# An offline-searched order of all instructions, butterflies over four row tiles, and final sums copied by ScalarE

## The chip, the cores and the metric

The kernel runs on one core of one Trainium2 chip. The metric is the device time of one execution in microseconds (us), given as the median of several executions on the same chip. The span in a profile runs from the first to the last instruction; in the runs of this case the time is 1.8 to 2.1 us longer than the span. The profile also gives the granted clock of TensorE, 1.00 being full rate. An execution is called slow when it is more than 1.5% above the fastest of its kernel; such executions are told, but not compared.

## The reference

```python
def reference(A_x, A_w_r, A_w_i, B_x, B_w_gate, B_w_up, B_w_down):
    xn = layernorm(A_x)                                  # x: 1 x 2048 x 640, bf16
    X = rfft2(xn.astype(float32)) * (A_w_r + 1j * A_w_i) # filter: 2048 x 321
    a = irfft2(X).astype(bfloat16)
    h = (xn @ B_w_gate) * (xn @ B_w_up)                  # 640 -> 1536
    return A_x + a + h @ B_w_down                        # 1536 -> 640
```

(The original has helpers for the Fourier transforms and makes random inputs.)

There are thus two branches on the same normalised x. The gate/up/down branch is plain matrix products. The spectral branch does the two-dimensional Fourier transform as a few stages: butterflies on VectorE, small products with tables on TensorE, a multiplication by the filter, and the same backwards.

## The kernel before

Every piece of work is a task: a name, the engines that can do it, an estimated duration for each, what it reads and writes, and a function that emits the instructions. A list scheduler in the program then decides order, engine and PSUM bank, always taking the task with the best priority among those that can start soon:

```python
def plan(self, nbanks=8, filler_deadline=0.0):
    ...
    while nsch < ntot:
        ...                                   # candidates: earliest start per engine
            slack = self.slack.get(e_, 100.0)
            ...
            for c in lst:
                if c is hc or c[1] <= hc[0] + slack:
                    k = (c[0], c[3].prio, c[3].tid)
        ...
        t.eng = e; t.start = est; order[e].append(t)
```

The order so found is emitted as it stands; each engine works through its list, and a task that has to wait holds up all behind it on its engine.

At the start 40 matmuls on zeros warm TensorE up, and "fillers" (four matmuls of 64 columns each) run where it would idle:

```python
dma("ld_sm0", v_sm[:, 0, :], d_sm[:, 0, :], 128 * 256, ..., prio=0.002, q="act")   # identity, 32 KB
...
for fi in range(opts.get("nfill", 70)):       # 11 of them find a place: 44 matmuls
    ...
nwarm = opts.get("nwarm", 10)                 # 4 * nwarm matmuls of 128 columns
```

The spectral stage, for each of 32 groups q: a product C, the multiplication by the filter on VectorE (WM), negated copies (NG, NS), and ten inverse products IA. The products of WM lie so that the stationary operand of eight of the ten takes every fourth element:

```python
def em_wm(...):                               # VectorE, 2 x 256 and 130 results
    xh = ps[:, bk, 0:256].rearrange("p (k h m) -> p h m k", k=4, h=2)[:, h]
    wv = wg[:, :, 0:320].rearrange("p w (m k) -> p w m k", k=10)
    wv = wv[:, :, :, 1:5] if h == 0 else wv[:, :, :, 9:5:-1]
    dst = yg[:, 578:1090].rearrange("p (w h m k) -> p h w m k", w=2, h=2, k=4)[:, h]
    c.e.tensor_tensor(dst, xh.unsqueeze(1).to_broadcast([128, 2, 32, 4]), wv, _OP.mult)
    ...
def em_ia(...):
    for k in range(5):
        if k < 4:
            l1, l2 = yg[:, 578 + k:1090:4], yg[:, 322 + k:834:4]
        else:
            l1, l2 = yg[:, 0:128], yg[:, 128:256]
        c.e.matmul(dst, l1, v_ti[:, q, 0, :], start=True, stop=False)
        ins = c.e.matmul(dst, l2, v_ti[:, q, 1, :], start=False, stop=True)
```

Butterflies go over two row tiles at a time, and each final sum is read from PSUM by VectorE, in two or three pieces for each of 16 row tiles:

```python
for g in range(8):
    b = 2 * g                                 # forward butterflies: 14 instructions a group
...
def em_f1(...):                               # FIN: PSUM + x -> out
    return c.e.tensor_tensor(v_out[:, a % 2, sl3], ps[:, bk, 0:n], v_xr[:, xs, sl3], _OP.add)
```

Of the kernel before, what the change touches and what calls it, by code (L numbers as in the profile page):

```python
# [17 lines left out]
_DMA_ISSUE = 500.0  # L18


class _Task(object):
    __slots__ = ("tid", "name", "engs", "dur", "emit", "prio", "deps", "nleft", "succ", "bank", "frees",
                 "freers", "eng", "start", "end", "seq", "units", "nbytes", "semkey", "semval", "cls", "vc",
                 "waits")
# [47 lines left out]
class _Sched(object):  # L72
    def __init__(self):
        self.tasks = []
        self.bufs = []
        self.caps = {}
        self.window = 250.0
        self.affinity = 600.0
        self.dma_bw = _DMA_BW
        self.slack = {"pe": 1000.0, "act": 300.0, "dve": 400.0, "pool": 100.0, "sp": 0.0}  # L80
        self.order = None
        self.urgent = ()
        self.makespan = 0.0
# [71 lines left out]
    def plan(self, nbanks=8, filler_deadline=0.0):  # L155
        tasks = self.tasks
        for t in tasks:
            t.succ = []
        for t in tasks:
            t.deps.discard(t)  # L160
            for d in t.deps:
                d.succ.append(t)
            t.nleft = len(t.deps)
        eng_free = dict((e, _START) for e in _ENGS)
        seq = dict((e, 0) for e in _ENGS)
        banks = [[0.0, None] for _ in range(nbanks)]
        held_by_cls = {}
        avail = [t for t in tasks if t.nleft == 0]
        pending_free = {}
        for t in tasks:  # L170
            if t.bank is not None:
                if not t.freers:
                    raise RuntimeError("task %s takes banks but nothing frees them" % t.name)
                pending_free[t.tid] = len(t.freers)
        free_end = {}
        dma_pipe = 0.0
        order = dict((e, []) for e in _ENGS)
        nsch = 0
        ntot = len(tasks)
        dropped = []  # L180

        def choose(kind):
            best = None
            if kind == "pair":
                for k in range(0, nbanks, 2):
                    a_, b_ = banks[k], banks[k + 1]
                    if a_[0] is None or b_[0] is None:
                        continue
                    ft_ = max(a_[0], b_[0])
                    if best is None or ft_ < best[0]:  # L190
                        best = (ft_, k)
            else:
                for k in range(nbanks):
                    st = banks[k]
                    if st[0] is None:
                        continue
                    partner = banks[k ^ 1]
                    pen = 0.0 if partner[0] is None else 1.0
                    key = (pen, st[0])
                    if best is None or key < best[2]:  # L200
                        best = (st[0], k, key)
            return best

        def release(p):
            k0 = p.units[1]
            nb = 2 if p.units[0] == "pair" else 1
            for k in range(k0, k0 + nb):
                banks[k][0] = free_end[p.tid]
                banks[k][1] = list(p.freers)
            held_by_cls[p.cls] -= 1  # L210

        while nsch < ntot:
            cands = []
            for t in avail:
                unit_choice = None
                bank_ready = 0.0
                if t.bank is not None:
                    cap = self.caps.get(t.cls)
                    if cap is not None and held_by_cls.get(t.cls, 0) >= cap:
                        continue  # L220
                    ch = choose(t.bank)
                    if ch is None:
                        continue
                    unit_choice = (t.bank, ch[1])
                    bank_ready = ch[0]
                    if bank_ready > 0.0:
                        bank_ready += _XLAT["pe"]
                best = None
                for ei, e in enumerate(t.engs):
                    est = eng_free[e]  # L230
                    for d in t.deps:
                        lat = _SLAT[e] if d.eng == e and not d.nbytes else _XLAT[e]
                        if d.eng == e and e == "pe":
                            lat = -_TAIL[e]
                        de = d.end + lat
                        if de > est:
                            est = de
                    if bank_ready > est:
                        est = bank_ready
                    fin = est + t.dur[e]  # L240
                    score = fin + (self.affinity if ei > 0 else 0.0)
                    if best is None or score < best[3]:
                        best = (est, fin, e, score)
                cands.append((best[0], best[1], best[2], t, unit_choice))
            real = [c for c in cands if c[3].cls != "fill"]
            if not cands or (not real and nsch + len([a_ for a_ in avail if a_.cls == "fill"]) < ntot
                             and not any(c[3].cls == "fill" for c in cands)):
                raise RuntimeError("scheduler deadlock: %d/%d scheduled, avail=%s" % (
                    nsch, ntot, [a_.name for a_ in avail][:10]))
            pick = None  # L250
            by_eng = {}
            for c in cands:
                by_eng.setdefault(c[2], []).append(c)
            for e_ in by_eng:
                lst = by_eng[e_]
                hb = None
                for c in lst:
                    k = (c[3].prio, c[0], c[3].tid)
                    if hb is None or k < hb[0]:
                        hb = (k, c)  # L260
                hc = hb[1]
                slack = self.slack.get(e_, 100.0)
                if hc[3].name in self.urgent:
                    slack = 100.0
                ch_ = None
                for c in lst:
                    if c is hc or c[1] <= hc[0] + slack:
                        k = (c[0], c[3].prio, c[3].tid)
                        if ch_ is None or k < ch_[0]:
                            ch_ = (k, c)  # L270
                c = ch_[1]
                k = (c[0], c[3].prio, c[3].tid)
                if pick is None or k < pick[0]:
                    pick = (k, c)
            est, fin, e, t, unit_choice = pick[1]
            if t.cls == "fill" and (est > filler_deadline or not real):
                for f in [a_ for a_ in avail if a_.cls == "fill"]:
                    avail.remove(f)
                    dropped.append(f)
                    nsch += 1  # L280
                    for s_ in f.succ:
                        s_.deps.discard(f)
                        s_.nleft -= 1
                        if s_.nleft == 0:
                            avail.append(s_)
                continue
            t.eng = e
            t.start = est
            if t.nbytes:
                issue_end = est + t.dur[e]  # L290
                ds = max(issue_end + _DMA_LEAD, dma_pipe)
                de = ds + t.nbytes / self.dma_bw
                dma_pipe = de
                t.end = de + _DMA_LAT
                eng_free[e] = issue_end
            else:
                t.end = fin + _TAIL[e]
                eng_free[e] = fin
                seq[e] += 1
            t.seq = seq[e]  # L300
            order[e].append(t)
            if unit_choice is not None:
                k0 = unit_choice[1]
                nb = 2 if unit_choice[0] == "pair" else 1
                for k in range(k0, k0 + nb):
                    st = banks[k]
                    if st[1] is not None:
                        for fr in st[1]:
                            t.deps.add(fr)
                    st[0] = None  # L310
                t.units = unit_choice
                held_by_cls[t.cls] = held_by_cls.get(t.cls, 0) + 1
            if t.bank is not None and t in t.freers:
                pending_free[t.tid] -= 1
                fe = free_end.get(t.tid, 0.0)
                if t.end > fe:
                    free_end[t.tid] = t.end
                if pending_free[t.tid] == 0:
                    release(t)
            for p in t.frees:  # L320
                pending_free[p.tid] -= 1
                fe = free_end.get(p.tid, 0.0)
                if t.end > fe:
                    free_end[p.tid] = t.end
# [8 lines left out]
        for f in dropped:  # L333
            self.tasks.remove(f)
# [48 lines left out]
_D = 640  # L383
# [966 lines left out]
```

## Time and profile before

| | before |
|---|---|
| time | 204.6 us (204.3 to 205.0), three executions |
| span of the profiled execution | 202.8 us, clock 1.00 |
| busy shares TensorE / VectorE / ScalarE / GpSimd | 98 / 89 / 63 / 16% |
| first 512-column product starts | 22.94 us |
| last matmul starts | 200.26 us |

The lines that carry the reading are in the prediction below.

### The profile page before, as it was taken

To read this page: it belongs to the slowest core of one execution; us is meant where nothing else is said; L and a number is where in the kernel's file an instruction comes from. 1 tells how busy PE (TensorE), PEld (TensorE's weight loads), DVE (VectorE), ACT (ScalarE), POOL (GpSimd) and SP (SyncE) were. 2 spreads that over 40 slices of the span, in tenths; PEclk is the share of its full clock that TensorE was granted. 3 is DMA by queue.
4 is the path that set the end of the run, shared out by engine and by line. 5 is a ranking of instruction groups with operands and counts; after the bars stand their busy time and mean duration, and the time that the engine had idled before them with its cause. 6 is when DMAs were issued, how large, how long until landed. Compare 5 with 4: busy or idle time off the path is not lost.

```text
span 202.8 us, 4769 instructions
## 1 busy us (share of the span) xinstructions
PE 198.0 (98%) x1785; PEld 128.1 (63%) x1785; DVE 179.5 (89%) x511; ACT 127.5 (63%) x277; POOL 32.0 (16%) x108
## 2 busy tenths in 40 slices
PE   7999999999999999899999999999999999999995
PEld 7987644454444555556666666667777767777774
DVE  3599999999999997697988898864999999999983
ACT  3678899999975776869999999987611220200000
POOL 0000000000000000075754675453000000000000
DMA  6999983031161597605354444004313332332222
GB/s 183 300 341 378 377 80 65 3 65 32 32 63 39 112 276 194 197 14 132 74 145 114 103 102 127 0 5 136 92 32 97 106 107 66 113 90 81 93 65 65
DMA packets 31542, 23.82 MB, mean 117 GB/s; under 512 B 10528, under 2 KB 29472, under 8 KB 31392
## 3 DMA queue, kind: packets, MB, share of 16 engines
q1 hardware_dynamic: 30720, 23.16, 43.5%
q10 hardware_dynamic: 800, 0.36, 0.6%
q8 instruction: 14, 0.23, 0.5%
q14 instruction: 8, 0.07, 0.1%
HBM read 18.92 MB, written 2.62 MB: 106 GB/s over the span
## 4 chain that ended last, share of the span: by engine, by line
PE 85%; DVE 5%; SPq 4%; DMA 4%; issue 1%; ACT 1%
PE ps L978 44%; PE ps L1237 23%; SPq L712 4%; DMA arena<-in_A_x_dram 4%; PE ps L1131 3%; PE ps L1130 3%; PE ps L998 2%; PE ps L1079 2%; PE ps L938 2%; PE ps L1159 2%; PE ps L1249 2%; PE ps L1056 2%; DVE arena L719 1%; DVE arena L1257 1%; DVE arena L1186 0%
## 5 line engine op out<-in xcount | busy, mean ns | idle before, releaser
L718 ACT ACTIVATE arena<-ps 128x512 bf16<-128x512 f32 (+7 forms) x206 | 104.8, 547 | 40.1 <-PE ps L1159 24.0
L978 PE MATMUL ps<-arena 128*128 128x512 bf16 x420 | 97.0, 379 | 0.1
L978 PEld LDWEIGHTS ps<-arena 128*128 128x128 bf16 x420 | 38.9, 98 | 41.9 <-ACT arena L718 1.4
L1237 PE MATMUL ps<-arena 128*128 128x320 bf16 (+2 forms) x396 | 56.5, 295 | 0.2 <-DVE arena L1257 0.2
L1237 PEld LDWEIGHTS ps<-arena 128*128 128x128 bf16 x396 | 37.6, 98 | 13.9 <-DVE arena L1257 0.5
L1094 DVE TENSOR_TENSOR arena<-ps,arena 128x256 bf16<-128x256 f32 x64 | 24.0, 416 | 0.1
L1014 DVE TENSOR_TENSOR arena<-arena 128x512 bf16<-128x512 bf16 x42 | 17.7, 421 | 4.7 <-ACT arena L718 4.7
L1107 POOL TENSOR_SCALAR arena<-arena 128x256 bf16<-128x256 bf16 x8 | 6.8, 855 | 89.3 <-DVE arena L1097 89.2
L719 DVE CAST arena<-ps 64x321 bf16<-64x321 f32 (+1 forms) x25 | 12.2, 490 | 6.3 <-PE ps L1131 5.8
L1257 DVE TENSOR_TENSOR arena<-ps,arena 128x320 bf16<-128x320 f32 (+2 forms) x33 | 15.4, 473 | 1.8 <-PE ps L1249 1.8
L998 PE MATMUL ps<-arena 128*128 128x128 bf16 (+1 forms) x160 | 14.4, 246 | 0.4 <-ACT arena L718 0.4
L1130 PEld LDWEIGHTS ps<-arena 128*128 128x128 bf16 x160 | 12.4, 114 | 2.8 <-ACT arena L718 0.4
L998 PEld LDWEIGHTS ps<-arena 128*128 128x128 bf16 x160 | 12.0, 98 | 2.1 <-ACT arena L718 1.2
L1130 PE MATMUL ps<-arena 128*128 128x64 bf16 x160 | 13.3, 196 | 0.0
L1131 PE MATMUL ps<-arena 128*128 128x64 bf16 x160 | 13.3, 197 | 0.0
L1131 PEld LDWEIGHTS ps<-arena 128*128 128x128 bf16 x160 | 11.2, 113 | 2.1
L1116 POOL TENSOR_SCALAR arena<-arena 128x65 bf16<-128x65 bf16 x32 | 12.1, 378 | 0.0
L1114 POOL COPY arena<-arena 128x63 bf16<-128x63 bf16 x32 | 8.6, 268 | 17.1 <-DVE arena L1097 17.0
L1097 DVE TENSOR_TENSOR arena<-ps,arena 128x130 bf16<-128x130 f32 x32 | 9.3, 292 | 0.0
L776 ACT ACTIVATE arena<-arena 128x640 bf16<-128x640 bf16 x11 | 9.1, 824 | 0.0
L1115 POOL COPY arena<-arena 128x63 bf16<-128x63 bf16 x32 | 9.0, 280 | 0.0
L891 DVE TENSOR_TENSOR arena<-arena 128x384 f32<-128x384 bf16 x16 | 8.8, 552 | 0.0
(62 smaller groups left out, 221.0 us busy)
## 6 DMA issues: line engine op xcount, KB each, us to landing
arena<-in_A_x_dram SPq DMA_DIRECT2D x20, 160.0 KB, 2.4
out_dram<-arena SPq DMA_DIRECT2D x31, 80.0 KB, 1.6
arena<-in_A_w_r_dram SPq DMA_DIRECT2D x8, 160.5 KB, 3.0
arena<-in_A_w_i_dram SPq DMA_DIRECT2D x8, 160.5 KB, 3.0
arena<-in_B_w_gate_dram SPq DMA_DIRECT2D x4, 320.0 KB, 5.8
arena<-in_A_x_dram SPq DMA_DIRECT2D x1, 1280.0 KB, 9.8
arena<-in_A_w_r_dram SPq DMA_DIRECT2D x14, 80.2 KB, 2.9
arena<-in_A_w_i_dram SPq DMA_DIRECT2D x14, 80.2 KB, 3.1
```

Of the source, the lines that this page charges most:

```text
L718: return c.e.activation(dst, src, _ACTF.Copy)
L719: return c.e.tensor_copy(dst, src)
L978: ins = c.e.matmul(ps[:, bk, :], v_gw[:, w, j, ft, :], v_xt[:, j, rows], start=(j == 0), stop=(j == 4))
L998: ins = c.e.matmul(ps[:, bk, w * n:(w + 1) * n], v_gw[:, w, j, ft, :], v_xt[:, j, rows], start=(j == 0), stop=(j == 4))
L1014: return c.e.tensor_tensor(v_ht[:, ft0, rows], v_gbf[:, rr, 0, :], v_gbf[:, rr, 1, :], _OP.mult)
L1094: c.e.tensor_tensor(dst, xh.unsqueeze(1).to_broadcast([128, 2, 32, 4]), wv, _OP.mult)
L1097: return c.e.tensor_tensor(d5, x5, wg[:, :, 0:321:5], _OP.mult)
L1116: return c.e.tensor_scalar(yg[:, 128:193], yg[:, 256:321], -1.0, None, _OP.mult)
L1130: c.e.matmul(dst, l1, v_ti[:, q, 0, :], start=True, stop=False)
L1131: ins = c.e.matmul(dst, l2, v_ti[:, q, 1, :], start=False, stop=True)
L1237: ins = c.e.matmul(ps[:, bk, 0:sl3.stop - sl3.start], v_ht[:, ft, a * 128:(a + 1) * 128], v_wd[:, ft, sl3], start=(ft == _FT_ORDER[0]), st ...
L1257: return c.e.tensor_tensor(v_out[:, a % 2, sl3], ps[:, bk, 0:sl3.stop - sl3.start], v_xr[:, xs, sl3], _OP.add)
```

## The change

The intent is to stop scheduling by priorities. A search done beforehand, with durations fitted to measured ones, gave a table with one entry for each of 1021 tasks; the program replays it. With it come tasks that unload VectorE, and a leaner start.

```diff
-    def plan(self, nbanks=8, filler_deadline=0.0):
-        ...
+    def replay(self, plan):
+        for tid, ei, bk in plan:
+            t = by.pop(tid)
+            e = _ENGS[ei]
+            ...                               # banks: wait for whoever frees bank bk
+            order[e].append(t)
+_PLAN = ( (14, 4, -1), (178, 1, -1), (8, 2, -1), ... )   # task, engine, bank; cut
@@ butterflies
-        for g in range(8):
-            b = 2 * g
+_S_GROUPS = ((0, 2), (2, 2), (4, 4), (8, 4), (12, 4))
+        for g, (b, nt) in enumerate(opts.get("s_groups", _S_GROUPS)):
@@ layer norm: mean subtraction and scale in one instruction for rows 4 to 15
+                    return c.e.tensor_scalar(v_x[:, b, :], v_x[:, b, :], mean, v_rs[:, b:b + 1], _OP.subtract, _OP.mult)
@@ final sums, rows 0 to 14
-                    c.e.tensor_tensor(v_out[...], ps[...], v_xr[...], _OP.add)            # VectorE
+                T("FINA_%d_%d" % (a, hf), "act", ...)   # ScalarE: PSUM -> out, frees the bank
+                    return c.e.tensor_tensor(v_out[:, a % 2], v_out[:, a % 2], v_xr[:, xs, :], _OP.add)
@@ start
-        for fi in range(opts.get("nfill", 70)):
+        for fi in range(opts.get("nfill", 3)):
-        nwarm = opts.get("nwarm", 10)
+        nwarm = opts.get("nwarm", 9)
```

(The other butterfly stages change alike; epsilon is added through the bias of the square root; the statistics of row 1 move to VectorE; the estimated durations are new.) The table also holds the order of the loads. On ScalarE's queue the up weights (task 178, 320 KB) now come ahead of the identity (task 0, 32 KB).

## The prediction

> **What bounds the kernel now.** I read the page first: busy shares, chain, groups.
>
> ```profile
> PE 198.0 (98%) x1785; PEld 128.1 (63%) x1785; DVE 179.5 (89%) x511; ACT 127.5 (63%) x277; POOL 32.0 (16%) x108
> ...
> PE 85%; DVE 5%; SPq 4%; DMA 4%; issue 1%; ACT 1%
> ...
> L978 PE MATMUL ps<-arena 128*128 128x512 bf16 x420 | 97.0, 379 | 0.1
> ...
> L1237 PE MATMUL ps<-arena 128*128 128x320 bf16 (+2 forms) x396 | 56.5, 295 | 0.2 <-DVE arena L1257 0.2
> ```
>
> TensorE is busy 98% and holds 85% of the chain that ended last; its two big groups (gate/up products, down products) have almost no idle time. But busy does not say how fast: a matmul's record includes its pipeline tail (379 ns for 512 columns). So next, the chain in order of time, and the timeline of the start:
>
> ```profile
> 25.82 7.55 PE ps L978 x35
> ...
> 193.39 4.48 PE ps L1237 x33
> ```
>
> ```profile
> 5.55 0.69 PE L849 MATMUL ps<-arena 128*128 128x128 bf16 x5
> ...
> 6.03 1.84 PE L738 MATMUL ps<-arena 128*128 128x64 bf16 x44
> ...
> 7.71 1.28 PE L998 MATMUL ps<-arena 128*128 128x128 bf16 x20
> ...
> 18.25 4.86 PE L998 MATMUL ps<-arena 128*128 128x256 bf16 x40 [0.40 <-ACT arena L718]
> ...
> 200.52 0.29 DVE L1257 TENSOR_TENSOR arena<-ps,arena 128x128 bf16<-128x128 f32 x1 [0.30 <-PE ps L1249]
> ```
>
> 7.55 us / 35 = 215.7 ns per 512 columns and 4.48 / 33 = 135.8 ns per 320: back to back. I therefore took every matmul's start from the trace and compared the distance to the next with columns / 2.4 + 2.4 ns. All matmuls at that rate need 192.15 us; from the first start (1.04) to the end of the last they take 199.4. The 7.3 us between are: 2.9 before 8 us (half-rate warm-up, waits for the first rows), 1.2 between 8 and 24 us (0.56 at 17.6 where evictions stood behind statistics that waited for x), none from 24 to 80, 2.5 from 80 to 144 (0.71 at 84.2, 0.31 at 93.2, the rest in pieces under 0.1), 0.4 at 163, 0.2 at the end. Besides, 44 filler matmuls (1.68 us) run at 6.03 while the real ones wait. So the kernel is bound by the number of columns through TensorE, and only 6.1 us after the first transpose at 5.55 are not work: columns of work 188.6, 5.55 + 188.6 + 6.1 = 200.3, where the last matmul stops issuing. Then 2.5 us of last addition and store to the span of 202.8; the time is 1.8 more (204.6).
>
> The table by stretches shows how close the others are:
>
> ```profile
> 24.00:80.00 56.00, 56.00 (x316) 27.22 (x315) 55.67 (x166) 46.91 (x100) 0.00 (x0) 1.00 0.46 89
> 80.00:144.00 64.00, 63.24 (x752) 39.88 (x749) 50.99 (x154) 57.67 (x130) 31.83 (x104) 1.00 0.39 104
> 144.00:200.00 56.00, 55.82 (x450) 41.07 (x449) 54.39 (x131) 6.74 (x11) 0.00 (x0) 1.00 0.27 79
> ```
>
> Columns after the width: TensorE, weight loads, VectorE, ScalarE, GpSimd. VectorE is full in the first (forward butterflies) and last stretch (inverse butterflies, final sums), ScalarE nearly full in the middle one, nearly idle in the last. They keep up, but just.
>
> **The Trainium skill.** "TensorE: Matmul & The Clock Gate", section "Back-to-back issue gap", gives N/2.4 + 2.5 ns warm: the trace agrees (215.7 ns for 512). The same section's 131 ns for 512 columns in a stream with weight loads is not what this trace does. The same page, "What's actually happening": about 3.4 us of activity before full rate. Here the first five transposes at 5.6 us still step at 107 ns, the fillers at 6.03 at full rate (29 ns for 64 columns). "VectorE: DVE Perf Modes", "Mode 1× (REGULAR) — the baseline": fp32 with two tensors gives one result per cycle; at the page's 0.96 GHz that is 533 ns for 512. Start to start the trace has 600 ns for 512 (L1206) and 335 for 256, so about 67 ns are fixed per instruction. "DMA: Bandwidth & Descriptors", "Queues, rings and completion order": SP and ACT feed rings on the same 16 engines, so reordering the first loads does not add bandwidth.
>
> **The change, part by part.**
>
> *TensorE.* The order of the built program has the same real matmuls; only 4 warm-up and 32 filler matmuls go. The floor stays 188.6 us. Everything below matters only as far as it removes part of the 6.1 us, or brings the first transpose forward.
>
> *Start.* The addition of epsilon leaves VectorE (bias of the square root): about 0.2 us less before the first transpose, 5.55 to about 5.34. Row tile 1's statistics leave ScalarE, so the first evictions are not behind them; three fillers of four remain instead of eleven. The transpose at the cold rate ends about 6.05; VectorE then copies after row 1's statistics (to 6.5); first product about 6.55 instead of 7.71. But the third unit of products needs the second pair of gate/up loads, whose last landing in the trace is at 8.6. Both kernels have two units and two transposes ahead of it; now it starts at 9.1, then at 8.65: a gain of 0.45 us, not 1.2. Beyond, two transposes move and statistics of x come later in ScalarE's order: walking VectorE and ScalarE with measured steps (statistics 0.40, subtract and scale 0.30, product 0.34, eviction 0.49) I find no wait up to 21.3 us, where the first 512-column product would start (now 22.94 + stall 0.2). Gain by there: 0.45 + 1.05 of stalls = **1.5 us**.
>
> *VectorE.* Forward butterflies: 8 x 14 = 112 instructions become 5 x 14 = 70; inverse 8 x 13 = 104 become 65. Merging two of 256 into one of 512 saves 2 x 335 - 600 = 70 ns: 42 x 0.07 + 39 x 0.07 = 5.7 us. Mean subtraction fused for 12 rows: 12 x 0.30 = 3.6. Epsilon and copies of statistics: about 1.5. Final sums: 33 x about 0.40 = 13.3 become 15 bf16 additions of 640 (about 0.40) and 3 direct ones, 7.0: 6.3 less. Against that it takes over 7 evictions of 512 (0.60), 2 + 4 of 640 (0.74), one row's statistics (0.9), and gives back 3: about +8.8. Net -8 us, but none of it on TensorE's path by itself.
>
> *ScalarE.* 30 copies of 320 at 0.32 = +9.6 us, in a stretch where it is idle; about as much given away elsewhere.
>
> *Order.* The spectral stage begins after 210 matmuls of 512 columns instead of 255: 45 x 0.216 = 9.7 us earlier, so products are left to fill the later stages. Forward butterflies must then be done by about 71 us. From 20.8 us VectorE has about 48.7 us of work up to there in 50.3: 97%. Here is the tight place. In the spectral stage ScalarE falls from 50 to about 44 us of work, VectorE about 49, in 54: better balanced, so the 2.5 us should shrink.
>
> *Tail.* The same three last pieces, directly: still 2.5 us. Half as many stores, off the path.
>
> Sum: 204.6 - 1.5 (start) - 2.9 (the waits of now between 80 and 164 us) + s, where s is what the new order has of its own after the start: 200.2 + s.
>
> **Rivals.** (1) *Perfect recovery*, s about 0.2: 200.4. For it: durations in the plan equal the measured steps (0.600 us for 512 fp32 elements, 0.394 for statistics), so the search saw the right machine. (2) *New small waits*: s 1 to 2, so 201 to 202. A plan without margin in strict order stops TensorE at each eviction that is 50 ns late; the old plan had longer assumed durations (105 ns fixed on ScalarE) as hidden margin and still lost 2.5. VectorE at 97% up to 71 us belongs here. (3) *VectorE or GpSimd becomes the bound*: negations on GpSimd go from 8 to 15 at 0.8 us, each ahead of an inverse product; if that chain or the butterflies are late by 2 to 3 us, 203 and no gain. GpSimd is at 32 of 64 us there, so I doubt it. (4) *It is all hidden*: 2% is 4.1 us, and only 6.1 exist, 1.6 of which are nailed by the loads at 8.6 us.
>
> **Range and chances.** I take s = 0.7: **200.9 us**. Range 199.6 (all recovered, and the first loads 0.5 us earlier) to 202.6 (s about 2.4). The border of 2% is 200.5, s = 0.3, a little below my middle; I give faster 0.40, within 2% 0.59, slower 0.01.
>
> **What would show it.** Right: same 188.6 us of columns; third unit's first matmul near 8.65; first 512-column product near 21.3; first spectral matmul near 71 with a wait under 0.5 us before it; no VectorE fullness in the last stretch; ScalarE filling there. Wrong: the excess over the rate staying above 3 us after 24 us, TensorE waiting for VectorE between 60 and 72 us or for GpSimd in the spectral stage; or, the other way, loads landing earlier than 8.6 us or waits of nearly nothing after it, giving under 200.

## More of the kernel before

One more view of the kernel before belongs here, the waits of TensorE: which operation waited for which engine, the total in us, how often, and the longest. It lists only the larger ones.

```profile
PE ps L749 <- DVE arena L730: 1.0, 1, 1.0
PE ps L1079 <- DVE arena L719: 0.5, 1, 0.5
PE ps L998 <- ACT arena L718: 0.4, 1, 0.4
PE ps L1237 <- DVE arena L1257: 0.2, 1, 0.2
```

The first is the start itself (warm-up waits for a memory to be zeroed). The other three add up to 1.1 us.

## The result, and the profile after

| | before | changed |
|---|---|---|
| time, first comparison | 204.8 (204.3 to 205.0), 4 runs | 203.5 (202.7 to 203.8), 4 runs |
| time, second chip session | 205.0 (204.5 to 205.8), 12 runs | 203.3 (202.8 to 203.65), 6 runs |
| ratio to before, 95% interval | | 0.9928 [0.9899, 0.9957]; 0.992 [0.9894, 0.9945] |

A ratio is the mean time of one kernel's fast runs over that of the kernel before in the same rounds, so not quite the ratio of the medians above. The change makes the kernel 0.7 to 0.8% faster. The class (within 2%) was given the larger chance, but the time was predicted as 200.9 with 202.6 at the most, and it is 0.9 us outside that range.

The page of the changed kernel, first its busy line, then the chain that ended last by engine, then the groups of gate/up and of down products (busy us, mean ns of one, and idle time before):

```profile
PE 196.4 (97%) x1749; PEld 128.2 (64%) x1749; DVE 172.8 (86%) x396; ACT 128.7 (64%) x284; POOL 37.0 (18%) x116
...
PE 95%; DVE 2%; DMA 1%; issue 0%; ACT 0%
...
L948 PE MATMUL ps<-arena 128*128 128x512 bf16 x420 | 98.5, 379 | 0.0
...
L1206 PE MATMUL ps<-arena 128*128 128x320 bf16 (+2 forms) x396 | 58.1, 295 | 0.0
```

VectorE lost 6.7 us (8 were predicted) and 115 instructions; ScalarE took 1.2 us more. TensorE's share of the chain went from 85 to 95%. From this page the change looks like a full success. The table by stretches (width, then TensorE, weight loads, VectorE, ScalarE, GpSimd, clock) agrees:

```profile
24.00:80.00 56.00, 55.97 (x369) 28.60 (x367) 54.54 (x113) 49.86 (x109) 3.35 (x9) 1.00 0.52 116
80.00:144.00 64.00, 63.98 (x721) 40.79 (x720) 57.06 (x150) 47.00 (x105) 33.34 (x103) 1.00 0.30 82
144.00:200.00 56.00, 55.54 (x431) 39.54 (x429) 42.63 (x76) 17.66 (x40) 0.00 (x0) 1.00 0.26 82
```

In the last stretch VectorE went from 54.4 of 56 us to 42.6, and ScalarE from 6.7 to 17.7. The distances between the starts of matmuls confirm the rest. After 24 us the kernel before had waits of 0.71, 0.31, 0.05, 0.24, 0.34 and 0.07 us, 1.7 in all. The changed one has 0.20, 0.18, 0.15 and 0.14 us, 0.7 in all.

In this execution the loss is at the start. TensorE in order of time, the changed kernel:

```profile
3.78 0.76 PE L720 MATMUL ps<-arena 128*128 128x128 bf16 x10
5.97 0.44 PE L818 MATMUL ps<-arena 128*128 128x128 bf16 x5 [1.44 <-DVE arena L798]
6.25 0.40 PE L709 MATMUL ps<-arena 128*128 128x64 bf16 x8
7.24 1.23 PE L968 MATMUL ps<-arena 128*128 128x128 bf16 x10 [0.59 <-ACT arena L775]
```

The warm-up ends at 4.4, but the first transpose starts at 5.97, not at the predicted 5.34, after 1.6 us without an issue; two groups of fillers follow, and then TensorE has no issue for 0.75 us more. The next ten matmuls of 128 columns then take 1.23 us where 0.72 would do. The same thing by one-us stretches, where the third number from the end is the granted clock:

```profile
6.00:7.00 1.00, 0.65 (x13) 0.52 (x13) 0.97 (x4) 0.48 (x2) 0.00 (x0) 1.00 1.21 292
7.00:8.00 1.00, 0.77 (x8) 0.80 (x9) 0.84 (x4) 0.20 (x1) 0.00 (x0) 0.63 1.19 298
8.00:9.00 1.00, 1.00 (x14) 1.00 (x12) 0.00 (x0) 0.38 (x1) 0.00 (x0) 0.50 1.07 334
9.00:10.00 1.00, 1.00 (x12) 1.00 (x11) 0.76 (x3) 0.00 (x0) 0.00 (x0) 0.50 1.19 302
10.00:11.00 1.00, 1.00 (x15) 1.00 (x14) 0.87 (x4) 0.38 (x1) 0.00 (x0) 0.67 1.20 290
```

TensorE ran at half rate from about 7.25 to 10.66 us, 3.4 us in all. (The column also reads 1.00 in the first microseconds, where the matmuls of the warm-up start 107 ns apart, half rate; only later changes are recorded.) The first 512-column product started at 23.00, as late as before (22.94), instead of 21.3. This execution took 203.84 us, 2.9 more than predicted, and 1.7 of these are lost before the first large product. In two of the first four executions the granted clock averages 0.99 (203.6 and 203.8 us), in the others it is 1.00 (202.7 and 203.4).

### The profile page after: what moved, and what is told of

The parts are those of the page before. It is cut to its first block, busy times and chain, and to the rows that moved or that the text cites. A ratio compares the mean times of both kernels' runs of the same rounds, so it can differ in the third digit from the quotient of the medians.

```text
span 201.8 us, 4578 instructions
## 1 busy us (share of the span) xinstructions
PE 196.4 (97%) x1749; PEld 128.2 (64%) x1749; DVE 172.8 (86%) x396; ACT 128.7 (64%) x284; POOL 37.0 (18%) x116
## 4 chain that ended last, share of the span: by engine, by line
PE 95%; DVE 2%; DMA 1%; issue 0%; ACT 0%
PE ps L948 45%; PE ps L1206 26%; PE ps L968 7%; PE ps L1100 3%; PE ps L1101 3%; PE ps L1026 2%; PE ps L908 2%; PE ps L1129 2%; PE ps L1049 2%; PE ps L1218 2%; DMA arena<-in_A_x_dram 1%; DVE arena L756 1%; PE ps L818 1%; DVE arena L765 0%; DVE arena L798 0%; DVE arena L792 0%
## 5 line engine op out<-in xcount | busy, mean ns | idle before, releaser
L685 ACT ACTIVATE arena<-ps 128x512 bf16<-128x512 f32 (+7 forms) x225 | 109.1, 528 | 61.0 <-PE ps L1218 30.1
L948 PE MATMUL ps<-arena 128*128 128x512 bf16 x420 | 98.5, 379 | 0.0
L948 PEld LDWEIGHTS ps<-arena 128*128 128x128 bf16 x420 | 39.6, 98 | 40.0 <-ACT arena L685 0.7
L1206 PE MATMUL ps<-arena 128*128 128x320 bf16 (+2 forms) x396 | 58.1, 295 | 0.0
L1206 PEld LDWEIGHTS ps<-arena 128*128 128x128 bf16 x396 | 37.7, 98 | 14.5
L1077 POOL TENSOR_SCALAR arena<-arena 128x256 bf16<-128x256 bf16 x15 | 12.8, 859 | 75.8 <-DVE arena L1067 75.8
L686 DVE CAST arena<-ps 64x321 bf16<-64x321 f32 (+3 forms) x31 | 17.2, 556 | 2.6 <-PE ps L1101 0.9
L1245 DVE TENSOR_TENSOR arena<-arena 128x640 bf16<-128x640 bf16 x15 | 7.4, 491 | 10.8 <-ACT arena L685 10.7
L968 PE MATMUL ps<-arena 128*128 128x128 bf16 (+1 forms) x160 | 15.2, 261 | 0.6 <-ACT arena L775 0.6
L968 PEld LDWEIGHTS ps<-arena 128*128 128x128 bf16 x160 | 13.5, 106 | 1.5 <-DMA arena<-in_B_w_gate_dram 0.7
L1100 PEld LDWEIGHTS ps<-arena 128*128 128x128 bf16 x160 | 12.0, 114 | 1.7 <-DVE arena L686 0.3
L1101 PEld LDWEIGHTS ps<-arena 128*128 128x128 bf16 x160 | 11.3, 114 | 0.9
L1084 POOL COPY arena<-arena 128x63 bf16<-128x63 bf16 x32 | 8.3, 260 | 11.5 <-DVE arena L1067 11.4
L1026 PEld LDWEIGHTS ps<-arena 128*128 128x128 bf16 x160 | 7.4, 98 | 3.7 <-ACT arena L685 0.4
L1218 PE MATMUL ps<-arena 128*128 128x320 bf16 (+2 forms) x33 | 8.6, 295 | 0.0
L1026 PE MATMUL ps<-arena 128*128 128x64 bf16 (+1 forms) x160 | 8.5, 193 | 0.0
```

Of the source, the lines that this page charges most:

```text
L685: return c.e.activation(dst, src, _ACTF.Copy)
L686: return c.e.tensor_copy(dst, src)
L948: ins = c.e.matmul(ps[:, bk, :], v_gw[:, w, j, ft, :], v_xt[:, j, rows], start=(j == 0), stop=(j == 4))
L968: ins = c.e.matmul(ps[:, bk, w * n:(w + 1) * n], v_gw[:, w, j, ft, :], v_xt[:, j, rows], start=(j == 0), stop=(j == 4))
L1026: ins = c.e.matmul(ps[:, bk, k * 64:k * 64 + n], v_uq[:, k, t, :], v_fd[:, k * 128 + w * n: k * 128 + w * n + n], start=True, stop=True)
L1077: return c.e.tensor_scalar(yg[:, 322:578], yg[:, 834:1090], -1.0, None, _OP.mult)
```

## The experiments

Three causes were on the table. **S**: the start (late x, idle TensorE, clock). **P**: the "pieces under 0.1 us" of the kernel before, which the change was expected to remove, are no waits at all. **A**: a delay on ScalarE behind the start. The rival to all was that the remaining waits after 24 us are larger than they look.

### The start: e1_order, e2_busy, e3_both, after_again

Three versions of the changed kernel. One puts the identity back ahead of the up weights; one gives back warm-up and filler matmuls; one does both.

```diff
 e1_order: the identity's load (task 0) first on ScalarE's queue
-    (14, 4, -1), (178, 1, -1), ... (9, 3, -1), (0, 1, -1),
+    (14, 4, -1), (0, 1, -1), ... (9, 3, -1), (178, 1, -1),
 e2_busy: 40 warm-up and 36 filler matmuls instead of 36 and 12
-        nwarm = opts.get("nwarm", 9)
+        nwarm = opts.get("nwarm", 10)
-                for i in range(4):
+                for i in range(12):
 e3_both: both edits
```

> The changed kernel, but ScalarE's queue issues the 32 KB identity before the 320 KB up load again, as the kernel before did. Theory A (the swapped loads delay the first rows): first rows land near 3.2 us instead of 3.73, second rows near 4.2 instead of 5.29, first transpose near 5.45 instead of 5.97, first 512-column product 0.5 to 1.2 us earlier than 23.0, time 0.5 to 1.2 us lower (about 202.5). Theory B (only the idle TensorE and its clock matter): the landings may move, but as long as the half-rate stretch after 7 us is there in some runs, the time stays within 0.3 us of the changed kernel's 203.4.

> The changed kernel with 40 instead of 36 warm-up matmuls and three times as long fillers (36 instead of 12 small matmuls), loads as in the changed kernel. Theory B: no half-rate stretch after 7 us in any run (granted clock 1.000 in all of them), so about 0.5 us less on average, 203.0 or lower, and a smaller scatter. Theory A: the clock may be steady but the first rows still land at 3.7, so the gain is at most 0.5 us and the first 512-column product stays above 21.8 us.

> Both: loads of ScalarE's queue in the old order and the longer warm-up and fillers. If A and B are both causes, the first 512-column product starts near 21.4 us, the time is 1.5 to 1.8 us below the changed kernel: 201.6 to 201.9, clock 1.000 in all runs. If it stays above 202.5, something else in the start is missing from both.

After these, the changed kernel itself was run again, to see whether its lower clock is its own or the first chip session's.

> The changed kernel, unchanged, once more on another chip. Theory S (start): with only 36 warm-up and 12 filler matmuls TensorE idles while it waits for x, and in some executions the granted clock drops; I expect a median of 203.3 us, between 202.7 and 203.9, a spread of over 0.8 us, with mean granted clock 0.99 in the long executions and 1.00 in the short ones. Rival: the 0.99 of the first chip was a trait of that chip; then all executions here have 1.00 and lie within 0.3 us.

| | median us (fast runs) | ratio to before | clock in fast runs | first 512-column product (profile) |
|---|---|---|---|---|
| after_again | 203.32 (202.80 to 203.65) | 0.992 | 1.00 x4, 0.992 x2 | 21.45 |
| e1_order | 202.80 (202.68 to 203.17) | 0.9895 | 1.00 in all | (slow run) |
| e2_busy | 202.97 (202.79 to 203.03) | 0.9901 | 1.00 or 0.999 | 21.73 |
| e3_both | 202.83 (202.52 to 203.06) | 0.9894 | 1.00 in all | 21.32 |

The last column needs care. In these three profiles the record of the first 512-column product itself is missing, and the first one recorded starts 0.22 us later. The weight loads are complete. In after_again there are five of them for four recorded products, and the first load stands where the product before it starts:

```profile
20.79 0.82 PE L968 MATMUL ps<-arena 128*128 128x256 bf16 x6
21.66 1.03 PE L948 MATMUL ps<-arena 128*128 128x512 bf16 x4
...
21.34 0.85 PEld L948 LDWEIGHTS ps<-arena 128*128 128x128 bf16 x5
```

So the missing product started at 21.45, one product (216 ns) ahead of 21.66.

The clock drop is the changed kernel's own: two of six executions again had 0.992, and both lie at 203.6 us; one at 203.65 had 1.00, so the drop is not all of its spread. With either edit no fast execution (17 in all) shows it, and the median falls by 0.35 to 0.5 us, the spread to between 0.2 and 0.55 us. (The intervals of single ratios overlap. For e1_order alone five executions without the drop show little, where four of ten had it before.) Three of the four executions of after_again at full clock, 202.8 to 203.0 us, are about as fast as the mended ones: what the start costs in time is mainly the drop. In the table by stretches of after_again the same idle stretch as above is followed by full rate, so the idle stretch does not always cost:

```profile
7.00:8.00 1.00, 0.89 (x18) 0.92 (x19) 0.72 (x3) 0.21 (x2) 0.00 (x0) 1.00 1.19 299
8.00:9.00 1.00, 1.00 (x19) 0.87 (x17) 0.56 (x2) 0.39 (x2) 0.00 (x0) 1.00 1.07 334
```

e1_order also had one execution of 228.7 us at a mean clock of 0.854. It was the one profiled, so that profile only tells that x rows 0 and 1 landed at 3.16 and 4.21 us again and the first transpose started at 5.41.

More important is what the clean starts do not give: e3_both was expected at 201.6 to 201.9, its first 512-column product came at 21.32 as hoped, and 202.8 us is still 1.9 above the prediction. Theory S alone is not enough.

### The two halves of it in the kernel before: e4_before_swap, e5_before_nofill

```diff
 e4_before_swap: the kernel before, identity after the up weights
-dma("ld_sm0", ..., prio=0.002, q="act")
+dma("ld_sm0", ..., prio=0.006, q="act")
 e5_before_nofill: the kernel before, 36 warm-up and 12 filler matmuls
-        for fi in range(opts.get("nfill", 70)):
+        for fi in range(opts.get("nfill", 3)):
-        nwarm = opts.get("nwarm", 10)
+        nwarm = opts.get("nwarm", 9)
```

> The kernel before with one thing of the change done alone: on ScalarE's queue the up weights (320 KB) load ahead of the identity (32 KB). Theory: that order alone delays x rows 0 and 1 (from 3.2 and 4.1 to about 3.5 and 5.1 us) and the first transpose (5.5 to about 6.0 us); its 40 + 44 filler matmuls keep the clock up; time 0.2 to 0.5 us longer than before, up to 205.5. Rival: x lands as before and the delay in the changed kernel came of something else; then the time is within 0.1 us of before.

> The kernel before with 36 warm-up and 12 filler matmuls instead of 40 and 44, nothing else. Theory: by itself the loss of fillers brings the gate/up products forward (the 44 took 1.84 us at 6.03 while rows were awaited), but if TensorE idles for long enough the clock falls to half in some executions, as in the changed kernel; x lands earlier here, so the idle stretch ahead of the first transpose is about 1.1 us instead of 1.6, and I expect the drop in few executions or none: time 204.5 to 205.0 with clock 1.00, or up to 205.8 in executions with clock 0.99. Rival: the clock falls after any idle of 0.7 us: then all executions have 0.99.

Both took 204.62 us against 205.08 for the kernel before, ratios 0.9986 [0.9972, 0.9999] and 0.998 [0.9966, 0.9994]. So neither costs anything there, and the expectation for the first, up to 0.5 us longer, was wrong. In its profile x row 0 does land later (3.57 us instead of 3.20) and the first transpose does start later (5.91 instead of 5.55), but the first 512-column product starts at 22.89 as ever (22.94 before, 22.88 in the second): in the kernel before, what follows up to 23 us absorbs it. One of six executions of e5_before_nofill had a clock of 0.992. The clock drop thus occurs with few fillers and early x too; whether late x makes it likelier is not shown. What the kernel before has and the changed one lacks is room after the start: between 8 and 24 us it has 1.2 us of waits that take up a late beginning, the changed one in after_again under 0.2.

### The pace of the inverse products: e7_contig

In the kernel before the excess between 80 and 144 us was 2.54 us: 1.3 in four waits above 0.05, and 1.2 in pieces. The changed kernel still has 1.2 us of such pieces. Nearly all of them (1.1 us) lie at the inverse products. This version reads 128 neighbouring elements for every stationary operand. The result is wrong on purpose.

```diff
-                            l1, l2 = yg[:, 578 + k:1090:4], yg[:, 322 + k:834:4]
+                            l1, l2 = yg[:, 578 + 128 * k:706 + 128 * k], yg[:, 322 + 128 * k:450 + 128 * k]
```

> Wrong result on purpose: the changed kernel, but the inverse products of the spectral stage read their 128 stationary columns side by side instead of every fourth element. Theory C (the strided weights set the pace of these 64-column products: 33 to 34 ns, where the two of ten with contiguous weights take 29): all ten at 29 ns, about 1.1 us less in the sum of that group, time 0.5 to 1.1 us lower than the changed kernel. Rival (the pace comes from waits for evictions): 33 ns and the time stay.

Its time is 202.3 us (202.0 to 202.8, and one execution of 203.3 at clock 0.992), ratio 0.9878 [0.9852, 0.9903]. By the ratios that is 0.9 us below the changed kernel, whose start it has. But the changed kernel had the clock drop in two of six executions, this one in one. Among executions at full clock the medians are 202.94 and 202.23, so 0.7 us, and the profiled spans are 200.9 and 200.2. The first and last inverse products of one group, TensorE in order of time, first in the changed kernel, where L1026 is the next product:

```profile
105.47 0.19 PE L1100 MATMUL ps<-arena 128*128 128x64 bf16 x1
...
105.77 0.19 PE L1101 MATMUL ps<-arena 128*128 128x64 bf16 x1
105.80 0.31 PE L1026 MATMUL ps<-arena 128*128 128x64 bf16 x5
```

and in e7_contig:

```profile
104.36 0.19 PE L1100 MATMUL ps<-arena 128*128 128x64 bf16 x1
...
104.62 0.19 PE L1101 MATMUL ps<-arena 128*128 128x64 bf16 x1
104.65 0.31 PE L1026 MATMUL ps<-arena 128*128 128x64 bf16 x5
```

From first to next product is 0.33 us against 0.29, with no wait in either. Over all groups the median distances between strided products are 33 to 35 ns in the changed kernel and in the kernel before, and 29 throughout here. Summed over the thirty-two groups, the distances are 1.1 us more than 29 ns each in both kernels, and 0.1 us more here. So this pace is in both kernels, and the change never touched it. Not all of it turns into time: between 80 and 144 us e7_contig has 0.4 us more in waits than after_again, so that it gains 0.6 to 0.9 us and not 1.0.

### ScalarE behind the start: e9_x4

With a clean start three waits show up in e3_both, and in after_again, that the profiled changed kernel, being late, does not have: 0.16, 0.18 and 0.20 us at 31.0, 37.5 and 38.8 us, all for evictions by ScalarE. The first looks like 0.38 from start to start, and the expectation below still counts it so. But here too a matmul record is missing (0.22 us): the weight loads go on at 31.22, and not at the 31.45 of the next recorded product.

```profile
30.52 0.72 PE L908 MATMUL ps<-arena 128*128 128x128 bf16 x10
31.45 0.38 PE L948 MATMUL ps<-arena 128*128 128x512 bf16 x1 [0.21 <-ACT arena L685]
...
31.22 0.33 PEld L948 LDWEIGHTS ps<-arena 128*128 128x128 bf16 x3 [0.16 <-ACT arena L685]
```

ScalarE is full from 17 to 40 us, after an idle stretch in which it waits for x rows 4 to 7. Those are loaded behind the last pair of gate/up weights, so this version, on top of e3_both, loads them ahead.

```diff
 load order on SyncE's queue (tasks 183, 184: last pair of gate/up weights; 18: x rows 4 to 7)
-    183, 184, 18
+    18, 183, 184
```

> The changed kernel with the start mended (identity first, full warm-up and fillers) and, besides, x rows 4 to 7 loaded ahead of the last pair of gate/up loads. Theory A: ScalarE is idle until x rows 4 to 7 land at 16.9 us and then full to 40 us, and TensorE's waits at 31 to 39 us (0.76 us in all) are its evictions that come late. Then with x landing at about 13.6 us the waits at 31 to 39 shrink to under 0.3 us and the time is 0.5 to 0.8 us below that of the mended start alone (202.8): 202.0 to 202.3. Rival: the plan's order in strict sequence has other waits of the same size behind these (VectorE's statistics and subtractions of the same rows), and the time stays within 0.2 us of 202.8; or the gate/up loads, now later, stop the first 512-column products, and it is longer.

It took 202.49 us (202.22 to 203.10), ratio 0.9881 [0.9859, 0.9904], against 0.9894 for e3_both. ScalarE in order of time in e3_both, then in e9_x4:

```profile
12.44 3.13 ACT L685 ACTIVATE arena<-ps 128x256 bf16<-128x256 f32 x7
16.95 0.74 ACT L738 ACTIVATE arena<-arena 128x640 bf16<-128x640 bf16 x1 [1.38 <-DMA arena<-in_A_x_dram]
```

```profile
12.54 3.15 ACT L685 ACTIVATE arena<-ps 128x256 bf16<-128x256 f32 x7
15.59 0.73 ACT L738 ACTIVATE arena<-arena 128x640 bf16<-128x640 bf16 x1
```

The idle 1.38 us is gone (x lands at 14.5 instead of 16.9), and of the three waits 0.12 us is left. The gain in time is 0.3 us, less than the expected 0.5 to 0.8, which had counted the missing record as a wait. The three waits shrink by 0.42 us (0.54 to 0.12). Against that, the up weights of the second pair are 0.39 us late at 8.4 us, where e3_both waited 0.22. The profiled spans differ by 0.33. The waits show the cause; by the times alone 0.3 us is not clear of the scatter. (The same waits hide a late start: e2_busy starts its 512-column products 0.4 us later than e3_both, has 0.1 us of these waits, and takes only 0.14 us longer.)

### What the parts are worth: e6_list, e8_fin, e8_look

The first has the change's new tasks, but the order, engines and banks from the list scheduler of the kernel before. The second has the change's order with its final sums read from PSUM by VectorE again.

```diff
 e6_list
-        sch.replay(_PLAN)
+        sch.plan(8, filler_deadline=opts.get("fill_deadline", 7600.0))
 e8_fin
-                if a >= opts.get("fin_direct", 15):
+                if a >= opts.get("fin_direct", 0):
```

(In the second the table has VectorE's 33 sums in the places of the copies.)

> The change's new tasks (butterflies over four row tiles, fused mean subtraction, copies by ScalarE and half as many stores) with the order, engines and banks from the list scheduler of the kernel before. Theory O: what pays is the order; VectorE's 8 us less work was not on TensorE's path. Then this one loses about as much in waits after 24 us as the kernel before (1.7 us or more, as larger tasks are coarser to place) and takes 204 to 206 us. Rival theory W: the work taken from VectorE is what pays; then it takes 203.5 us or less, with waits after 24 us under 1 us.

> The changed kernel with one part undone: the final sums are read from PSUM by VectorE again, not copied by ScalarE (same order otherwise). VectorE gets about 6 us more work after 144 us, ScalarE about 9.6 us less. Theory: TensorE has no waits after 144 us in the changed kernel because VectorE has slack there; with 42.6 of 56 us busy it can take 6 more without a wait that matters; time within 0.4 us of the changed kernel. Rival: the copies are what removed the waits of 0.4 us at 163 us; then these or larger ones come back, 0.4 to 1 us longer.

e6_list took 212.4 us, ratio 1.036: the same tasks in the old way of ordering are 9 us slower than in the searched order, and 7.4 us slower than the kernel before. TensorE's waits in it:

```profile
PE ps L1131 <- ACT arena L716: 2.0, 2, 1.4
PE ps L849 <- DVE arena L829: 1.8, 3, 0.9
PE ps L1080 <- ACT arena L716: 1.8, 3, 1.0
```

Expected were 204 to 206, so this is a miss in size. VectorE has 12.5 us less work in it than in the kernel before (167.0 against 179.5), and by itself that is worth nothing. That coarser tasks are harder to place is the likely reason, but was not tested apart. The old scheduler's settings were tuned for the old tasks and not again, so how much of the 7.4 us tuning could recover is open.

e8_fin took 212.3 us in its fast runs, ratio 1.0355, where at most 1 us more than the changed kernel was expected: a clear miss. Its profile fell in an execution of 343.9 us at a clock of 0.56, which says nothing on the others.

> The kernel with final sums read by VectorE again, which took 212 us where 203 to 203.8 was expected, once more for a profile in the fast state (its profile fell in an execution at a clock of 0.56). Theory: in the plan's strict order VectorE's final sums, each waiting for a down product, stand ahead of the butterflies that release later TensorE work; TensorE then waits for VectorE between 130 and 190 us by 8 to 9 us in all. Rival: TensorE waits little and its products are paced slower (a clock below 1, as 0.98 to 0.99 in four of its executions); then the excess is spread over stretches without a releaser.

```profile
PE ps L1206 <- DVE arena L1227: 3.1, 2, 2.4
PE ps L1129 <- DVE arena L1186: 1.8, 1, 1.8
```

This is a single execution, at 211.95 us within the range of the fast ones. TensorE waits for VectorE 0.4, 2.0, 2.6 and 0.8 us at 150, 159, 171 and 198 us, 5.7 in all. After the longest the clock drops to half for 3.4 us (about 1.7 us lost), and the last matmul is followed by 4.4 us instead of 2.5 because VectorE's sums have queued up. Together that is the 9.3 us by which its span is longer than that of after_again; the theory, with 8 to 9 us of waits alone, was right in part. My expectation had added 6 us of VectorE's work (the page of this run has 178.1 us instead of 172.8, 5.3 more) to a stretch in which 13 of 56 us are free, and found room. But the room was spread over the stretch, and the sums sit in strict order ahead of butterflies that TensorE is waiting for. In this order the copies by ScalarE are not a nicety; they carry it.

### A correct version with a dense stationary operand: e10_lay, e12_write

If the pace of the inverse products costs 0.6 to 0.9 us, can a correct kernel have it back? Both versions build on e9_x4 and lay the filter's products out as [k][negated, first, second][64], so that both operands of a product are 128 neighbouring elements. In e10_lay VectorE's multiplication goes through them so that it writes neighbours, and reads the filter with a stride of 10 elements. In e12_write it reads as before, and writes with a stride of 192.

```diff
 both
-dst = yg[:, 578:1090].rearrange("p (w h m k) -> p h w m k", w=2, h=2, k=4)[:, h]
-l1, l2 = yg[:, 578 + k:1090:4], yg[:, 322 + k:834:4]
+dst = yg[:, 322:1090].rearrange("p (k j h m) -> p h j m k", k=4, j=3, h=2)[:, h, 1:3]
+l1, l2 = (yg[:, o + 192 * k:o + 192 * k + 128] for o in (386, 322))
 e10_lay besides: innermost m instead of k in all three operands
-xh, wv, dst: "... m k"
+xh, wv, dst: "... k m"
```

> The mended start and early x rows 4 to 7 (202.49 us), and besides the spectral products laid out so that the stationary operands of all ten inverse products are 128 contiguous elements; a correct result this time. Theory: the eight strided products go from 33 to 35 ns to 29 ns, as in the run with the wrong result; 32 groups x 8 x 4.5 ns is 1.1 us: time 201.3 to 201.7. VectorE's multiply writes contiguous rows now and reads the filter with a stride instead; if it stays within 5% of its duration nothing else changes. Rival: the strided read makes VectorE's multiply (or the negation) longer, and the waits of the spectral stage grow by what is gained: 202.2 or more.

> As e10_lay (mended start, early x rows 4 to 7, stationary operands of all inverse products contiguous), but VectorE's multiply goes through its elements in the order of the kernel before: it reads the filter as before and writes each product with a stride of 192 elements. Theory: the 609 ns of e10_lay came of the strided read of the filter; with the old order of reading the multiply is back at about 417 ns, the inverse products keep 29 ns, and the time is 0.9 us below e9_x4: 201.3 to 201.8. Rival: VectorE pays for a strided write as it did for the read (550 ns or more); then the time is 208 us or more, and the old layout, which puts the stride on TensorE's operand, is the cheaper place for it.

The results are right, and the inverse products keep 29 ns (in e12_write in the median). But the times are 211.05 and 251.8 us (ratios 1.0294 and 1.2303). VectorE's multiplications by shape, in e9_x4, e10_lay and e12_write (busy us, mean ns of one):

```profile
L1064 DVE TENSOR_TENSOR arena<-ps,arena 128x256 bf16<-128x256 f32 x64 | 24.0, 417 | 2.1 <-PE ps L1049 1.8
```

```profile
L1064 DVE TENSOR_TENSOR arena<-ps,arena 128x256 bf16<-128x256 f32 x64 | 36.3, 609 | 0.7 <-PE ps L1049 0.5
```

```profile
L1064 DVE TENSOR_TENSOR arena<-ps,arena 128x256 bf16<-128x256 f32 x64 | 78.3, 1416 | 0.7 <-PE ps L1049 0.5
```

The strided read adds 12 us to these multiplications, the strided write 54 us, in the stage in which VectorE has hardly any room. (In e12_write the third multiplication of each group, whose layout is unchanged, also grows from 293 to 507 ns, and all executions have a clock of 0.95 to 0.97; neither was followed up.) The rival named for each was right. Of the three layouts tried, that of the kernel before puts the stride where it costs least, on TensorE's operand. That this pace costs 0.6 to 0.9 us in time rests on e7_contig alone.

The best version found is e9_x4: 202.49 us, 1.2% faster than before and about 0.4% faster than the change as it came.

## Why the prediction was wrong

**Columns and bound: right.** The matmuls are the same, TensorE holds 95% of the chain, and nothing else became a bound.

**The order after 24 us: right in the profiled execution, in part by luck.** Waits of 1.7 us became 0.7 there, which is the s = 0.7 taken. But that execution was late. With a clean start (after_again) the waits after 24 us are 1.3 us. The last stretch has none, VectorE has room there, and ScalarE fills, as said.

**The step "2.5 from 80 to 144 (..., the rest in pieces under 0.1)", and with it "the waits of now between 80 and 164 us" of 2.9: wrong, the largest lasting miss.** About 1.1 us of the 2.9 is the pace of the inverse products, 33 to 35 ns instead of 29, which no order can remove. e7_contig shows it: with dense operands 1.0 us of the pieces is gone, and the time is 0.6 to 0.9 us less. The step had taken columns / 2.4 + 2.4 ns as the rate of all matmuls and called every excess a wait. The waits view, with 0.7 us of waits after 24 us in the kernel before, spoke against it (it counts from the modelled ends of matmuls; from start to start the waits were 1.7), and I did not lay the two side by side.

**The step "Start", first product about 6.55 and first 512-column product near 21.3: right in its sum where the clock stays up, wrong in its beginning and on the fillers.** In after_again the 512-column products begin at 21.45 instead of 22.94, a gain of 1.5 us, as summed. (22.94 less 1.5 is 21.4 and not the 21.3 that the prediction names.) But the step took 0.2 us off the first transpose for the work that left VectorE and did not look at the changed order of the loads: in three profiles with this start x row 0 landed at 3.4 to 3.7 us instead of 3.2, and the transpose moved from 5.55 to between 5.6 and 6.0, not to 5.34. With the loads in the old order (e1_order) it starts at 5.41. And it counted the removed fillers as a gain only. In four of the ten executions of the changed kernel the clock averages 0.99; in the profiled one it falls to half for 3.4 us and is most of the 1.7 us lost before the first large product. In time the drop is worth 1.0 us there (203.84 against 202.84) and 0.35 to 0.5 us in the median.

One reading in the prediction is off, without effect on its sums: the fillers at 6.03 did not all run at full rate. The first fifteen or so start 53 ns apart, and full rate begins at 6.9 us. That the order of the loads adds no bandwidth agrees with the runs: 300 GB/s in the first 20 us before, 295 in the changed kernel, 298 in e3_both.

**What was not seen at all:** "I find no wait up to 21.3 us" holds in after_again, but the walk ended there. Three waits for ScalarE at 31 to 39 us, 0.5 us together, follow from x rows 4 to 7 landing at about 17 us; e9_x4 shows it.

With these terms the sum closes for the execution of after_again with a clean start: 200.9 + 0 (start) + 1.1 (pace) + 0.5 (ScalarE) + 0.15 (other waits and pieces) + 0.15 (the time is 1.95 us longer than the span here, and was taken as 1.8) = 202.8; measured 202.84.

**The rivals.** "New small waits" was the nearest with 201 to 202, for the wrong reason: VectorE at 97% up to 71 us cost one wait of 0.2 us at 69.3. The range was too narrow above because the 2.9 us of "waits" were taken as certain.

## What to carry to other kernels

Before counting an excess over a rate as waits, check it per kind of instruction: a steady pace of one kind looks the same in the sum, and no order removes it. The view that lists waits by releaser should then add up to what remains; here it gave 0.7 us, and the distances at single places 1.7, where 2.9 had been assumed. When a change cuts warm-up or filler work, time it several times and look at the clock of each execution: fewer fillers cost nothing in the kernel before, and together with the swapped loads 0.35 to 0.5 us in the median of the changed one. Before reading a distance between matmuls as a wait, count the weight loads there: a missing record looked like a wait of 0.22 us twice. Free time of an engine over a long stretch says nothing about a strict order: 5 us of work more in a stretch with 13 us free cost 9 us.

## What the Trainium skill lacked or had wrong

- "TensorE: Matmul & The Clock Gate", section "Back-to-back issue gap": 131 ns for 512 columns in a stream with weight loads is not what these runs show (215.7 ns); its N/2.4 + 2.5 ns holds for operands that lie densely. It gives no price for the layout of the stationary operand: with every fourth bf16 element, products of 64 columns start 33 to 35 ns apart, with dense ones 29 ns.
- "SBUF — State Buffer", section "Door 1: The DMA port swizzle (why `[64,N]` ≈ `[32,N]`)", in its note on cachelines, says that two hits per line of 16 bytes absorb the latency, which would make every fourth bf16 element free. For TensorE's stationary operand it was not (33 to 35 against 29 ns). For VectorE the note points the right way: innermost steps of 10 elements in the read took the 256-element multiplication from 417 to 609 ns, steps of 192 elements in the write to 1416 ns.
- "VectorE: DVE Perf Modes", section "Mode 1× (REGULAR) — the baseline": it counts one result per cycle and lists "weird strides" among what works, without a price. For the bf16 filter and products these steps had one, the same 609 and 1416 ns for 256 results. (Elsewhere the skill does measure such steps, for 32-bit words.)
- "TensorE: Matmul & The Clock Gate", section "What's actually happening": the clock falls after an idle window of about 3.4 us. Here idle stretches of 1.6 and 0.75 us, with 0.5 us of work between them, went with a drop in four of the ten executions of the changed kernel (in the profiled one, half rate for 3.4 us), and one of 2.6 us did in e8_look. That the phase varies from run to run agrees.
- No page tells of whole executions of a one-core program at a low clock: 228.7 us at a mean of 0.854 (e1_order, one of six) and 343.9 us at 0.56 (e8_fin, one of six).
